# Three row blocks of the gate and up products in one 768-column pass of seven products ahead of the attention, and the down products issued one at a time

## The chip, the cores and the metric

One core of one Trainium2 chip runs the program; the other cores are idle. The metric is the device time of one execution in microseconds (us), and the median of several runs is compared. TensorE (PE) multiplies matrices: it loads a 128x128 stationary tile and streams columns past it (here up to 512 in one matmul) into PSUM, an on-chip accumulator of which the kernel uses eight banks of 512 f32. VectorE (DVE), ScalarE (ACT) and GpSimd (POOL) work on elements; SyncE (SP) issues most of the DMA transfers. Engines run their own instruction lists in order and wait for each other by semaphores.

## The reference, cut to what matters

```python
xn = layernorm(x)                                  # x: 2048 x 512
q  = xn @ wq                                       # 32 heads of 128
o  = softmax(q @ k_cache.T / sqrt(128)) @ v_cache  # per head, 2048 keys
s  = concat(o) @ wo                                # 4096 -> 512
gate, up = xn @ W_gate, xn @ W_up                  # 512 -> 1792 each
h  = relu(gate) * up
g  = silu(h @ W_down)                              # 1792 -> 512
out = x + s * g
```

All inputs are bf16. The two branches (attention s and gated network g) both start from the same normalised rows xn.

## The kernel before, in words

**Row blocks and chunks.** The 2048 rows are four blocks of 512, Q = 0 to 3. The 1792 inner columns of the gated network are FC = 14 chunks of 128. xnT holds xn transposed, with the 512 features as DC = 4 pieces of 128 on the partitions.

**Seven products in place of eight.** Most matrix products are done by Winograd's form of Strassen's method: a 2x2 block product from seven block products (numbered 1 to 7 in the code) instead of eight, with sums of the operands formed beforehand. For the gated network a unit is one chunk k: its gate and up weights are the two rows of the 2x2 scheme (`gu_sums` forms the four weight sums on POOL), two row blocks "lo" and "hi" are its two columns, and the row sums TX (`emit_tx`, on DVE) are shared with the query projection. Each product is two matmuls, one for each half of the feature pieces.

**Order of the work.** Block 0 comes first, plainly (eight matmuls of 512 columns for each chunk): `emit_gate_up(0)`, then `emit_down` with 4 x 14 matmuls, while the layer norm of the other blocks runs in its shadow (`ln_task`, `ln_finish`). Block 2 follows plainly, `emit_gate_up(2)`: 14 chunks x 8 matmuls of 512 columns. Then the attention starts: 32 heads x 4 row blocks make 128 blocks b of eight pairs p. For a pair, PE forms two score tiles (`emit_S_tile`, two matmuls of 512 columns, line 1648), ACT takes the exponential of both (line 1660, 128x1024), and three pairs later PE multiplies with the values (`emit_PV_tile`, eight matmuls of 129 columns, line 1757). Between pairs the list `plan` puts other work of PE: an item takes one of the three two-bank slots of PSUM that the score tiles also use (`emit_M`, `ring_acquire`). Blocks 1 and 3 of the gate and up products are such items: `emit_gu` (line 1199), 14 x 7 products, each 2 matmuls of 512 columns, in attention blocks 2 to 11. Every product is evicted from PSUM by itself: DVE adds it to a running sum (`comb`, line 1205). POOL multiplies gate and up (`gu_h`, lines 1175 and 1177). The weights are loaded a second time, chunk by chunk (`gu_load`), scaled on ACT (`gu_scale`) and summed on POOL.

**Down products.** Blocks 1, 2 and 3 take `emit_d`: seven products, each 14 matmuls of 256 columns (line 1260), in four items of 2, 2, 2 and 1 products. Their places were written by hand in `dplan`: block 2 at attention blocks 0 and 1, block 1 at 12 and 13, block 3 at 14 and 15. `emit_hs` (DVE) forms the sums of h for them, `emit_wd_scale` and `emit_wd_sums` those of W_down.

**Buffers.** Many buffers lie on top of one another in memory and are freed by waits. SP issues DMAs strictly in the order written.

Of the kernel before, what the change touches and what calls it, by code (L numbers as in the profile page):

```python
# [52 lines left out]
def bass_recurrent_scan__mha_block_cached__glu_gated_reglu__prompt_kernel(  # L53
# [63 lines left out]
    with ExitStack() as es:  # L117
# [18 lines left out]
        xnT = S_([128, DC, S], BF16, "xnT")  # L136
# [20 lines left out]
        QT_sb += [at_(xnT_at - base[0] + S + i * 2 * NQ, [128, NQ], BF16, "QT_sb") for i in range(2)]  # L157
# [11 lines left out]
        Wg_sb = at_(67584, [128, DC, F], BF16, "Wg_sb")  # L169
        Wu_sb = at_(81920, [128, DC, F], BF16, "Wu_sb")  # L170
# [4 lines left out]
        def sm_(shape, dt, name):  # L175
# [27 lines left out]
        uB = [at_(61952 + 1024 * i, [128, NQ], BF16, "uB") for i in range(2)]
        gA = [at_(o, [128, NQ], BF16, "gA") for o in (66560, 98304)]
        gB = at_(108544, [128, NQ], BF16, "gB")
        dbuf = {Q: [at_(o, [128, 2, D // 2], F32, "dbuf") for o in os_] for Q, os_ in (
            (2, tuple(range(0, 12288, 2048))), (1, o_w2 + o_sg))}
        dbuf[3] = dbuf[1]
# [20 lines left out]
        hlN = [at_(o, [128, 4, D], BF16, "hlN") for o in (88064, xnT_at - base[0] + 12288)]  # L229
# [18 lines left out]
        sem_gua = newsem()  # L248
        sem_hp = newsem()
# [95 lines left out]

        load_x0(sp, 0)
# [106 lines left out]

        def ln_norm(eng, sem, n, ctok):
            _wait(eng, ctok)
            return sem.sig(
                eng.tensor_scalar(xn_sb[:, n, :], x_sb[:, n, :], rstd[:, n, 0:1], nmr[:, n, 0:1],
                                  op0=ALU.mult, op1=ALU.add))
# [122 lines left out]
        def ln_finish(Q):  # L581
            ns, sqtok = ln_hold.pop("sq")
            ctok = ln_coef(ns, sqtok)
            for n in ns:
                ntok = ln_norm(pool, sem_nm, n, ctok)
                _wait(sp, ntok)
                xt_tok = sem_xq[Q].sig(
                    sp.dma_start_transpose(xnT[:, :, n * 128:(n + 1) * 128], xn_sb[:, n, :]))
# [31 lines left out]
        def emit_tx(k):  # L620
# [3 lines left out]
            b11, b12 = xnT[:, 0:HC, lo], xnT[:, 0:HC, hi]  # L624
            b21, b22 = xnT[:, HC:DC, lo], xnT[:, HC:DC, hi]
# [27 lines left out]
        def gu_scale(k):
            W = W2[k % NW]
            _wait(act, gu_tok[(k, "w")])
            wflat = W[:].rearrange("p c i e -> p (c i e)")
            gu_tok[(k, "s")] = sem_w2s.sig(act.activation(wflat, wflat, ACTF.Copy, scale=GSC))

        def gu_sums(k):
            W, X = W2[k % NW], SG[k % NW]  # L660
            if (k, "s") not in gu_tok:
                gu_scale(k)
            _wait(pool, gu_tok[(k, "s")])
            _wait(pool, gu_tok.get((k - NW, 4)))
            a11, a12 = W[:, 0:HC, 0, :], W[:, HC:DC, 0, :]
            a21, a22 = W[:, 0:HC, 1, :], W[:, HC:DC, 1, :]
# [10 lines left out]
        def emit_sw(pr):  # L677
# [3 lines left out]
            if pr == 0:  # L681
                _wait(pool, tx_tok[(1, 3)])
# [13 lines left out]
            if pr == 1:  # L696
                _wait(pool, glu_done_tok)
# [16 lines left out]
        def finish_gate_up(Q, fc, s, gtok, gu_tok):  # L714
# [4 lines left out]
            rtok = sem_relu.sig(  # L719
                act.activation(gr_sb[gk][:], g_ps, ACTF.Relu, scale=1.0 if Q == 0 else HSC))  # L720
            _wait(dve, gu_tok)
            _wait(dve, rtok)
            h_tok = sem_h.sig(
                dve.tensor_tensor((hT0 if Q == 0 else hT[1])[:, fc, :], gr_sb[gk][:], u_ps, ALU.mult)
            )
            h_done[(Q, fc)] = h_tok
            gr_free[gk] = h_tok
            if s is None:
                (acc_free if Q == 2 else y_bank_free)[:] = [h_tok, h_tok]
            else:  # L730
                ring_tok[s] = [rtok, h_tok]
            if Q == 0:
                ln_task(fc)
            return h_tok

        def emit_gate_up(Q):
            qs = slice(Q * NQ, (Q + 1) * NQ)
            h_tok = None
            for fc in range(FC):
                fs = slice(fc * 128, (fc + 1) * 128)  # L740
                if Q == 0 and fc < HFC:
                    s = half_slots[fc]
                    finish_gate_up(Q, fc, s, half_tok[(fc, 0)], half_tok[(fc, 1)])
                    continue
                if (Q, fc) in ((0, HFC), (2, FC - 2)):
# [4 lines left out]
                g_ps, u_ps = gu_banks(s)  # L750
# [1464 lines left out]
```

## Time and profile before

| what | value |
|---|---|
| median of 3 runs | 1233.03 us (1232.87 to 1233.4) |
| span of the profiled execution, first to last instruction | 1231.4 us |
| own time of the profiled execution | not listed; its span is 1.6 us below the median of the runs |
| PE busy | 1215.4 us (99%) |
| ACT busy | 1043.7 us (85%) |
| DVE busy | 874.6 us (71%) |
| POOL busy | 835.0 us (68%) |
| granted TensorE clock | 1.000 |

Busy time is the time in which an engine executes something. The chain of waits (part 4 of the page) follows the work that ended last back to its start; the view by windows gives busy time of each engine in a stretch; the groups of instructions give the mean duration of one. Mean durations of matmuls are not the pace of a stream: a 512-column matmul is listed with 379 ns, because its end is modelled behind the start of the next. Pace is read from the start times.

### The profile page before, as it was taken

To read this page: it belongs to the slowest core of one execution; us is meant where nothing else is said; L and a number is where in the kernel's file an instruction comes from. 1 tells how busy PE (TensorE), PEld (TensorE's weight loads), DVE (VectorE), ACT (ScalarE), POOL (GpSimd) and SP (SyncE) were. 2 spreads that over 40 slices of the span, in tenths; PEclk is the share of its full clock that TensorE was granted. 3 is DMA by queue.
4 is the path that set the end of the run, shared out by engine and by line. 5 is a ranking of instruction groups with operands and counts; after the bars stand their busy time and mean duration, and the time that the engine had idled before them with its cause. 6 is when DMAs were issued, how large, how long until landed. Compare 5 with 4: busy or idle time off the path is not lost.

```text
span 1231.4 us, 29085 instructions
## 1 busy us (share of the span) xinstructions
PE 1215.4 (99%) x11716; PEld 817.4 (66%) x11926; DVE 874.6 (71%) x1322; ACT 1043.7 (85%) x1114; POOL 835.0 (68%) x945
## 2 busy tenths in 40 slices
PE   9999999999999999999999999999999999999998
PEld 5466666776666666666666666666666666666665
DVE  7668787667676776677666776677676767676587
ACT  4367877668899999999999999999999999999994
POOL 3355876313767867787688776986788767668368
PEclk9999999999999999999999999999999999999999
DMA  9712431323223544246522854265522662248616
GB/s 278 158 31 33 81 80 25 52 48 94 54 52 52 142 125 126 49 94 173 174 38 52 211 155 94 50 154 151 155 52 51 184 191 48 53 104 161 128 35 142
DMA packets 285061, 127.21 MB, mean 103 GB/s; under 512 B 253696, under 2 KB 279552, under 8 KB 280064
## 3 DMA queue, kind: packets, MB, share of 16 engines
q1 hardware_dynamic: 283584, 124.55, 43.2%
q8 instruction: 95, 1.56, 0.6%
q10 hardware_dynamic: 1344, 0.79, 0.2%
q14 instruction: 38, 0.31, 0.1%
HBM read 57.93 MB, written 25.17 MB: 67 GB/s over the span
## 4 chain that ended last, share of the span: by engine, by line
PE 97%; issue 1%; POOL 1%; ACT 0%; DVE 0%; POOLq 0%; DVEq 0%
PE ps_acc L1757 37%; PE ps_r L1648 34%; PE ps_r L1081 5%; PE ps_r L1199 3%; PE ps_r L1545 3%; PE ps_r L1260 3%; PE ps_r L945 2%; PE ps_r L764 2%; PE ps_r L760 2%; PE ps_r L1480 2%; PE ps_acc L863 1%; PE ps_r L1577 1%; PE ps_r L1576 1%; PE ps_r L503 0%; POOL s_acc L1614 0%
## 5 line engine op out<-in xcount | busy, mean ns | idle before, releaser
L1660 ACT ACTIVATE PT<-ps_r 128x1024 bf16<-128x1024 f32 x1024 | 990.5, 1024 | 123.8 <-PE ps_r L1648 109.6
L1757 PEld LDWEIGHTS ps_acc<-V_sb,PT 128*128 128x128 bf16 x8192 | 544.5, 98 | 225.2 <-issue 29.0
L1757 PE MATMUL ps_acc<-V_sb,PT 128*128 128x129 bf16 x8192 | 629.7, 220 | 1.0
L1648 PE MATMUL ps_r<-QT_sb,KT_sb 128*128 128x512 bf16 x1848 | 571.2, 379 | 9.5
L1086 DVE TENSOR_TENSOR UVR<-UVR,ps_r 128x512 f32<-128x512 f32 (+1 forms) x228 | 168.9, 756 | 96.7 <-PE ps_r L1081 91.9
L1648 PEld LDWEIGHTS ps_r<-QT_sb,KT_sb 128*128 128x128 bf16 x2048 | 159.1, 98 | 35.6 <-ACT PT L1660 32.1
L1411 DVE TENSOR_TENSOR s_acc<-s_acc,ps_r 128x1024 f32<-128x1024 f32 x108 | 131.5, 1219 | 27.3 <-PE ps_r L1480 19.3
L1427 DVE TENSOR_TENSOR s_acc<-s_acc,ps_r 128x512 f32<-128x512 f32 x152 | 101.0, 683 | 28.9 <-PE ps_r L1545 23.5
L1680 DVE TENSOR_TENSOR Onorm<-ps_acc,rz_sb 128x512 bf16<-128x512 f32 x127 | 87.8, 691 | 4.4
L1511 POOL TENSOR_TENSOR TI<-OX 128x512 f16<-128x512 f16 x38 | 43.1, 1156 | 69.9 <-issue 68.6
L1046 POOL TENSOR_TENSOR TI<-xn_sb 128x512 f16<-128x512 f16 x48 | 55.9, 1164 | 39.9 <-PE ps_r L1081 39.9
L1086 DVE TENSOR_TENSOR QT_sb<-UVR,ps_r 128x512 bf16<-128x512 f32 x72 | 49.5, 688 | 43.6 <-PE ps_r L1081 41.3
L1677 DVE RECIPROCAL rz_sb<-ps_acc 128x4 f32<-128x4 f32 x127 | 23.2, 183 | 72.4 <-PE ps_acc L1757 70.3
L1511 POOL TENSOR_TENSOR TI<-OT_store 128x512 f16<-128x512 bf16 (+1 forms) x38 | 45.7, 1224 | 32.9 <-PE ps_r L1545 16.1
L1354 POOL TENSOR_TENSOR WX<-Wo_sb 128x512 f16<-128x512 bf16 x7 | 8.1, 1158 | 81.1 <-DVE Wo_sb L1344 42.1
L1046 POOL TENSOR_TENSOR TI<-xn_sb,TI 128x512 f16<-128x512 f16 x48 | 56.0, 1166 | 0.0
L1046 POOL TENSOR_TENSOR TI<-xnT 128x512 f16<-128x512 bf16 x36 | 41.6, 1157 | 13.8 <-PE ps_r L1081 13.8
L1081 PE MATMUL ps_r<-TI,SI 128*128 128x512 f16 x126 | 47.8, 379 | 0.1
L1545 PE MATMUL ps_r<-TI,SI 128*128 128x512 f16 x114 | 43.2, 379 | 0.0
L1046 POOL TENSOR_TENSOR TI<-xnT,TI 128x512 f16<-128x512 bf16 x36 | 41.6, 1156 | 0.0
L1175 POOL TENSOR_SCALAR gB<-gB 128x512 bf16<-128x512 bf16 x14 | 20.8, 1487 | 30.3 <-DVE gB L1205 30.3
L1154 POOL TENSOR_TENSOR UVR<-UVR,UVR 128x512 f32<-128x512 f32 x24 | 29.8, 1274 | 11.7 <-DVE UVR L1086 11.7
(248 smaller groups left out, 1436.8 us busy)
## 6 DMA issues: line engine op xcount, KB each, us to landing
sums<-s_acc SPq DMA_DIRECT2D x20, 1024.0 KB, 4.6
s_acc<-sums SPq DMA_DIRECT2D x18, 1024.0 KB, 5.8
V_sb<-in_A_v_cache_dram SPq DMA_DIRECT2D x32, 512.0 KB, 4.3
Wq_sb<-in_A_wq_dram SPq DMA_DIRECT2D x16, 256.0 KB, 4.4
Wo_sb<-in_A_wo_dram SPq DMA_DIRECT2D x8, 512.0 KB, 3.8
out_dram<-g_sb SPq DMA_DIRECT2D x4, 512.0 KB, 4.7
KR<-sums SPq DMA_DIRECT2D x4, 512.0 KB, 4.5
OT_store<-Onorm SPq DMA_TRANSPOSE x127, 2.7
```

The costliest lines, as they stand in the source:

```text
L1046: return sem_ui.sig(pool.tensor_tensor(dst, x, y, o))
L1081: return sem_up.sig(pe.matmul(dst, lhs, rhs, start=start, stop=stop, skip_group_check=True))
L1086: dve.tensor_tensor(dst, x, ps, ALU.add))
L1199: ins = pe.matmul(ps_r[:, bank, :], L(i), R(i), start=(i == 0), stop=(i == HC - 1))
L1411: t = sem_opa.sig(dve.tensor_copy(dst, sb) if new[0] else dve.tensor_tensor(dst, dst, sb, op))
L1427: t = dve.tensor_tensor(dst, dst, sb, op)
L1511: return sem_oi.sig(pool.tensor_tensor(dst, x, y, o))
L1545: return sem_op.sig(pe.matmul(dst, lhs, rhs, start=start, stop=stop, skip_group_check=True))
L1648: ins = pe.matmul(ps_r[:, 2 * s + tt, :], KT_sb[h % 2][:, t * 128:(t + 1) * 128], QT_sb[qt_slot[(h, Q)]][:], start=True, stop=True)
L1660: act.activation(PT[pb][:], ps_r[:, 2 * s:2 * s + 2, :], ACTF.Exp, scale=scale / WSC)
L1680: dve.tensor_tensor(Onorm[ob][:], o_ap, rz_sb[:].to_broadcast([128, 4, Dh]), ALU.mult))
L1757: ins = pe.matmul(o_ap, PT[pb][:, tt, j * 128:(j + 1) * 128], V_sb[vb][:, t, 0:VW], start=(t == 0 and j % 2 == 0), stop=(t == KT - 1 and j ...
```

## The change

1. **One pass for three row blocks.** Blocks 1, 2 and 3 of the gate and up products are computed together, ahead of the attention. "lo" is block 1 and the first 256 columns of block 2, "hi" is block 3 and the other 256 of block 2, so a product is two matmuls of 512 and two of 256 columns. `emit_tz` forms the row sums TZ for the extra columns. The plain pass `emit_gate_up(2)` and the items of `emit_gu` in the attention are gone.
2. **Sums in PSUM.** Products 1, 6, 5 and 3 accumulate in one PSUM slot "A"; ACT copies the slot out after each (768 columns, f32, the last with relu). Products 7 and 4 share a slot "D", product 2 has a slot "C"; DVE adds the copies to them (`dv`, `gate_low`). DVE also takes the relu of the lower gate and the products gate * up (`gu_h`), which POOL did before. Slots are three of the ring and the two accumulator banks of the values.
3. **A written schedule.** Chunk k issues its product m at step 7k + off[m], so neighbouring chunks interleave; PE waits inside a chunk for ACT's copies and DVE's sums.
4. **Weights stay.** The weights loaded at the start are scaled in place (`gu_scale` during block 0) and used again; the 28 reloads are gone.
5. **Block 2's h goes out.** Its products go through two small buffers to DRAM (14 stores of 128 KB) and come back in one load (`reload_h`) in attention block 6.
6. **Down products** are issued one at a time at 21 places in attention blocks 0 to 15, in the order of blocks 1, 3, 2.
7. **Around it.** The four transposes of a row block become one; the loads of the first heads, of wq and wo are issued elsewhere; W_down is scaled on ACT in seven pieces; the steps of the first query projection are placed anew; the first three score pairs are issued inside the last steps of the pass, and the exponentials of pairs 0, 3 and 4 wait for buffers of the pass.

```diff
-                xt_tok = sem_xq[Q].sig(
-                    sp.dma_start_transpose(xnT[:, :, n * 128:(n + 1) * 128], xn_sb[:, n, :]))
+            xt_ready[Q] = [sem_xq[Q].sig(sp.dma_start_transpose(
+                xnT[:, Q].rearrange("p c (n q) -> p (c n) q", n=4),
+                xn_sb[:, 4 * Q:4 * Q + 4, :].rearrange("p n d -> p (n d)")))]
...
+        def gu_h(k, part, gate, up):
+            t = gu_tok
+            z = slice(part * NX, (part + 1) * NX)
+            _wait_all(dve, [t["g", part, k], t["u", part, k], t.get(("hz", k - 2))])
+            h_done[(3 if part else 1, k)] = sem_hp.sig(
+                dve.tensor_tensor(hT[part][:, k, :], gate[:, 0:NQ], up[:, 0:NQ], ALU.mult))
+            t["f", part, k] = sem_hp.sig(dve.tensor_tensor(hz[k % 2][:, z], gate[:, NQ:], up[:, NQ:], ALU.mult))
+            if part:
+                _wait_all(sp, [t["f", 0, k], t["f", 1, k]])
+                t["hz", k] = sem_hz[k % 2].sig(sp.dma_start(h_keep[k], hz[k % 2]))
+
+        def gate_low(k):
...
+            _wait_all(dve, [gu_tok[(k, 2)], gu_tok["a1", k], gu_tok.get(("f", 0, k - 2))])
+            gu_tok["c11", k] = c = sem_gud.sig(dve.tensor_tensor(
+                g[:], a1b[k % 2][:], gu_ps(s), ALU.add))
...
+            if k > 1:
+                gu_h(k - 2, 1, gB, uB[k % 2])
+            _wait(dve, c)
+            gu_tok["g", 0, k] = sem_gud.sig(dve.tensor_scalar(g[:], g[:], 0.0, None, op0=ALU.max))
...
+                for i in range(HC):
...
+                    for a, r in enumerate(R):
+                        ins = pe.matmul(ps(s)[:, a * NQ:a * NQ + (NX if a else NQ)], L(i), r, start=start and i == 0,
+                                        stop=stop and i == HC - 1, skip_group_check=True)
...
             if m == 1:
+                s = take("A")
...
+                t["a1", k] = cp(a1b[k % 2], s, mm(s, True, False), t.get(("c11", k - 2)))
+            elif m == 6:
...
+                _wait_all(pe, [t[(k, "x")], t["a1", k]])
+                t["a2", k] = cp(a2, s, mm(s, False, False), t.get(("c21", k - 2)))
+            elif m == 5:
...
+                _wait(pe, t["a2", k])
...
+                t["a3"] = cp(a3b, s, mm(s, False, False), t.get("c22"))
+            elif m == 3:
+                s = gu_held["A", k]
+                _wait(pe, t["a3"])
+                t["g", 1, k] = cp(gB, s, mm(s, False, True), t.get(("f", 1, k - 1)), relu=True)
...
             elif m == 7:
+                s = take("D")
+                t["u", 1, k] = t["c22"] = dv(uB[k % 2], a3b, s, mm(s, True, False), t["a3"], t.get(("f", 1, k - 2)))
             else:
+                s = gu_held["D", k]
+                _wait(pe, t["c22"])
+                t["u", 0, k] = t["c21", k] = dv(uA, a2, s, mm(s, False, True), t["a2", k], t.get(("f", 0, k - 1)))
+                give("D", t["c21", k])
+                gu_h(k, 0, gA[k % 2], uA)
...
+            if gp == 0:
+                _wait(act, gu_tok["c11", FC - 1])
+            if gp == NPB - 3:
+                _wait(act, sem_hp.cur())
+            if gp == NPB - 2:
+                _wait_all(act, [s_.cur() for s_ in sem_hz])
...
-        dplan = {2: ((0, 1), (1, 0), (1, 2), (1, 5)),
-                 1: ((12, 3), (13, 0), (13, 3), (13, 6)),
-                 3: ((14, 3), (15, 1), (15, 3), (15, 6))}
+        dpos = [(0, 2), (1, 5), (2, 5), (3, 4), (4, 5), (5, 0), (5, 5), (6, 5), (7, 3), (7, 6), (8, 5), (9, 0), (9, 5),
+                (10, 5), (11, 3), (11, 6), (12, 5), (13, 0), (13, 5), (14, 5), (15, 6)]
...
-        hlast = emit_gate_up(2)
...
+        off = {1: 0, 2: 2, 6: 3, 5: 6, 7: 8, 4: 11, 3: 12}
+        gseq = sorted((7 * k + off[m], k, m) for k in range(FC) for m in off)
...
+        for k in range(2, FC):
+            gside(7 * (k - 1) + 5, gu_sums, k)
...
+            gside(18 + 14 * i, emit_tx, i)
...
+            gside(7 * (2 + i) + 1, emit_wd_scale, i)
+        gside(100, emit_M, [(emit_st, 2, 0, 1, 0)])
+        for gp, t in enumerate((97, 98, 101)):
+            gside(t, emit_S_pair, gp)
...
+        emit_down(h_last, {
+            0: [(gu_scale, FC - 1), (gu_sums, 0), (emit_M, [(emit_st, 2, 0, 0, 0)]), (emit_tx, 4), (emit_tx, 5), (emit_tx, 6), (emit_tx, 7), (emit_tz,)],
+            2: [(gu_begin,), (gu_run, 0, 1)],
+            (3, "mid"): [(gu_sums, 1), (gu_run, 3, 4)]})
+        _wait_all(dve, [y_last["t"], sem_g.cur()])
+        gu_run(1, 3)
+        gu_run(4, 7 * FC - 1)
+        gu_end()
+        gu_run(7 * FC - 1, 7 * FC + 13)
```

More of the change, by code (lines that the diff above doesn't have):

```diff
@@ L155, in at_ @@
             return nc.alloc_sbuf_tensor_at(f"{name}_{_cnt[0]}", shape, dt, offset=base[0] + off)
-        QT_sb += [at_(xnT_at - base[0] + S + i * 2 * NQ, [128, NQ], BF16, "QT_sb") for i in range(2)]
+        QT_sb += [at_(xnT_at - base[0] + 12288 + i * 2 * NQ, [128, NQ], BF16, "QT_sb") for i in range(2)]
         HF = FC // 2
@@ L203, in bass_recurrent_scan__mha_block_cached__glu_gated_reglu__prompt_kernel @@
[L203 to L208, printed above, removed]
+        NX = NQ // 2
+        NP3 = NQ + NX
+        SG = [PT[2][:].rearrange("p a q -> p (a q)").bitcast(F16).rearrange("p (j i e) -> p j i e", j=4, i=DC // 2),
+              at_(99328, [128, 4, DC // 2, 128], F16, "SG")]
@@ L248, in bass_recurrent_scan__mha_block_cached__glu_gated_reglu__prompt_kernel @@
         sem_gua = newsem()
+        sem_tz = newsem()
+        sem_tws = newsem()
+        sem_hz = [newsem(16) for _ in range(2)]
+        sem_h2 = newsem(16)
         sem_hp = newsem()
@@ L456, in ln_norm @@
             return sem.sig(
-                eng.tensor_scalar(xn_sb[:, n, :], x_sb[:, n, :], rstd[:, n, 0:1], nmr[:, n, 0:1],
+                eng.tensor_scalar(xn_view(n), x_sb[:, n, :].rearrange("p (c d) -> p c d", c=DC), rstd[:, n, 0:1], nmr[:, n, 0:1],
                                   op0=ALU.mult, op1=ALU.add))
@@ L659, in gu_sums @@
         def gu_sums(k):
[L660 to L666, printed above, removed]
+            W, X = w_chunk(k), SG[k % 2]
+            _wait_all(pool, [gu_tok[(k, "s")], gu_tok.get((k - 2, 7))])
+            if k == 1:
+                _wait(pool, sem_g.cur())
@@ L857, in emit_down @@
                     pe.wait_ge(sem_wd.h, 16)
-                _wait(pe, y_bank_free[jb])
+                if j < 2:
+                    _wait(pe, y_bank_free[jb])
+                    yps = ps_acc[:, jb, 0:D]
+                else:
+                    if j == 2:
+                        s = ring_acquire()
+                    yps = ps_r[:, 2 * s + jb, 0:D]
                 ins = None
@@ L862, in emit_down @@
                         pe.wait_ge(sem_h.h, h_last_tok[1] - (FC - 1 - fc))
-                    ins = pe.matmul(ps_acc[:, jb, 0:D], hT0[:, fc, j * 128:(j + 1) * 128],
+                    if fc == 10 and (j, "mid") in between:
+                        for fn, *args in between[j, "mid"]:
+                            fn(*args)
+                    ins = pe.matmul(yps, hT0[:, fc, j * 128:(j + 1) * 128],
                                     Wd_sb[:, fc, :], start=(fc == 0), stop=(fc == FC - 1))
@@ L1320, in emit_d @@
-            p4 = prod(4, banks[0])
-            k = comb(y1, c_u, banks[0], ALU.subtract, waits=(p4, d_tok["u"], d_tok["y1"]))
-            d_done[Q] = k
-            out(y1, "y1", 1, 0, 0, k)
+                defer(2, tanh)
+                defer(3, mult)
+            if m == 1:
+                _wait_all(pe, [h_done[(Q, FC - 1)], wd_tok["scale"]])
+            if m == 6:
+                _wait_all(pe, [hs_tok[(Q, 1, 2)], wd_tok["s", 1]])
+            if m == 7:
+                _wait_all(pe, [hs_tok[(Q, 1, 0)], wd_tok["s", 2]])
@@ L1895, in at @@
             plan.setdefault((b, p), []).append(list(items))
-        for step, b, p in ((1, 0, 3), (2, 0, 5)):
-            at(b, p, (emit_st, 2, 0, 1, step))
         GB = G * QB
@@ L2019, in bass_recurrent_scan__mha_block_cached__glu_gated_reglu__prompt_kernel @@
+        side.setdefault((6, 0), []).append((reload_h,))
+        for b in range(2, NBLK):
+            pr, r = (b - 2) // 8 + 1, (b - 2) % 8
             o = osteps.get(b)
```

522 lines of the change are left out of this document (253 added, 269 removed).

## The prediction

> **What bounds the kernel now.** I read the page first: its shares by engine and the chain of work that ended last.
>
> ```profile
> span 1231.4 us, 29085 instructions
> PE 1215.4 (99%) x11716; PEld 817.4 (66%) x11926; DVE 874.6 (71%) x1322; ACT 1043.7 (85%) x1114; POOL 835.0 (68%) x945
> PE 97%; issue 1%; POOL 1%; ACT 0%; DVE 0%; POOLq 0%; DVEq 0%
> ```
>
> The chain is PE for 97% of the span. Then the windows, for the plain pass of block 2, the attention blocks with gate and up items, and the rest (columns: length, busy time of PE, its weight loads, DVE, ACT, POOL):
>
> ```profile
> 43.00:68.00 25.00, 24.89 (x116) 11.36 (x116) 20.79 (x31) 11.28 (x17) 15.24 (x8) 1.00 0.70 151
> 102.00:204.00 102.00, 101.10 (x849) 62.38 (x864) 82.80 (x138) 79.16 (x85) 72.82 (x80) 1.00 0.33 64
> 270.00:1210.00 940.00, 931.10 (x9434) 637.72 (x9602) 660.45 (x953) 859.84 (x892) 682.32 (x786) 1.00 0.45 107
> ```
>
> PE lacks 1% everywhere, at clock 1.00. The chain in order of time says what that is, beside the group of score tiles:
>
> ```profile
> 43.04 0.86 PE ps_r L760 x4
> 43.90 0.86 PE ps_r L764 x4
> ...
> 48.22 0.86 PE ps_r L760 x4
> ...
> 84.69 3.06 PE ps_r L1260 x28
> 87.75 0.45 PE ps_acc L1757 x8
> 88.20 0.05 issue
> ```
> ```profile
> L1648 PE MATMUL ps_r<-QT_sb,KT_sb 128*128 128x512 bf16 x1848 | 571.2, 379 | 9.5
> ```
>
> The gaps are pieces of 0.05 us, and the score tiles number 1848 of the 2048 that 1024 pairs issue: 200 lost records at 0.05 us are the 9.5 us of idle time. They are no stalls. PE is full from the first matmul to the tail, so two things alone move the time: work of PE that goes, and stalls of PE that come. Nothing taken from DVE, ACT, POOL or DMA pays by itself.
>
> **Pace of PE.** Six groups of four take 48.22 - 43.04 = 5.18 us: 0.2158 us for a 512-column matmul. 28 matmuls of 256 columns take 3.06 us: 0.1093 each, with a weight load for each of them.
>
> **Work removed and added on PE.** The plain pass of block 2 goes: 14 x 8 = 112 matmuls of 512, 24.17 us. The 196 matmuls of 512 for blocks 1 and 3 move out of the attention and cost the same. 196 matmuls of 256 columns come: 21.42 us. Down products are 21 x 14 matmuls before and after; query projection and scores don't change. Gain: 24.17 - 21.42 = 2.75 us, if nothing stalls. The pass is then 14 chunks of 14 x (0.2158 + 0.1093) = 4.55 us, 63.7 us in all. The gain cannot be larger: before has no PE idle time to recover.
>
> **The pass in steady state: VectorE.** Its load of one chunk, from these groups, and from starts in order of time:
>
> ```profile
> L1205 DVE TENSOR_TENSOR gA<-gcu,ps_r 128x512 bf16<-128x512 f32 x14 | 9.6, 687 | 5.8 <-PE ps_r L1199 5.1
> L1411 DVE TENSOR_TENSOR s_acc<-s_acc,ps_r 128x1024 f32<-128x1024 f32 x108 | 131.5, 1219 | 27.3 <-PE ps_r L1480 19.3 <-PE ps_r L1545 8.0
> L834 DVE TENSOR_TENSOR HS_sb<-hT 128x1024 f16<-128x1024 f16 x3 | 2.1, 684 | 0.0
> L834 DVE TENSOR_TENSOR HS_sb<-hT 128x768 f16<-128x768 f16 x3 | 1.7, 566 | 0.0
> L1023 DVE TENSOR_SCALAR Wq_sb<-Wq_sb 128x1024 bf16<-128x1024 bf16 x12 | 5.0, 419 | 0.0
> L630 DVE TENSOR_TENSOR xn_sb<-xnT 128x1024 f16<-128x1024 bf16 x2 | 1.4, 684 | 0.0
> ```
> ```profile
> 102.87 0.69 DVE L1205 TENSOR_TENSOR gA<-gcu,ps_r 128x512 bf16<-128x512 f32 x1
> 103.59 0.29 DVE L1218 TENSOR_SCALAR gA<-gA 128x512 bf16<-128x512 bf16 x1
> ...
> 122.05 0.68 DVE L1205 TENSOR_TENSOR uB<-gcv,ps_r 128x512 bf16<-128x512 f32 x1
> 122.65 0.68 DVE L1205 TENSOR_TENSOR gB<-gcv,ps_r 128x512 bf16<-128x512 f32 x1
> ```
>
> In a stream a 512-wide sum out of PSUM takes 0.60 us (122.05 to 122.65), though it lasts 0.68; a dependent successor starts after 0.72. Per column (1219 - 687)/512 = 1.04 ns, so 768 columns take 0.60 + 0.27 = 0.87. Three sums (products 2, 7, 4): 2.6. Gate times up, 16-bit in SBUF: (684 - 566)/256 = 0.46 ns a column, so 512 and 256 columns last 0.45 and 0.33; less 0.08 of overlap each 0.62, for two parts 1.25. The relu over 768: 0.29 + 256 x (419 - 293)/512 = 0.36, less overlap 0.28. One dependent start (sum of product 4, then its multiplication): 0.12. Together 4.25 us of the 4.55: 93%, where before VectorE had 20.79 of 25 and 82.80 of 102. The four row sums placed inside the pass add 4 x 0.65 = 2.6. So 14 x 4.25 + 2.6 = 62.1 against PE's 63.7: slack 1.6 us, 0.11 a chunk.
>
> That takes the SBUF ops at their quiet durations. Beside POOL they are not always quiet:
>
> ```profile
> L1218 DVE TENSOR_SCALAR gA<-gA x14: 293/418/633, 103.6 to 213.1; 128x512 bf16<-128x512 bf16 x14
> ```
> ```profile
> L1218 DVE TENSOR_SCALAR gA<-gA 128x512 bf16<-128x512 bf16 x14 | 6.3, 452 | 0.5
> L670 POOL TENSOR_TENSOR SG<-SG,W 128x256 f16<-128x256 f16 x14 | 9.8, 703 | 0.0
> L1177 POOL TENSOR_TENSOR hT<-gA,uA 128x512 f16<-128x512 bf16 x14 | 16.5, 1179 | 1.2 <-DVE uA L1205 1.1
> ```
>
> The relu of before took 293 to 633 ns, mean 452, where POOL was busy 73 of 102 us. In the pass POOL has only the weight sums, about 4 x 0.70 = 2.8 of 4.55 us, and by the order of waits they start at the end of product 7: while VectorE takes its two PSUM sums (which keep 687 beside POOL). I count one op hit in a chunk, 0.16 us: 14 x 4.41 + 2.6 = 64.3, 0.6 above PE. Bounds: 0 (none hit) and five ops hit, 5 x 0.16 = 0.8: 14 x 5.05 + 2.6 = 73.3, 9.6 above. I take 0.6, nearer to the lower end, because the two engines' bursts fall at different steps.
>
> [...] The spread of the relu agrees with an interference; its mean does not with a block for a whole op, 1.18 us for the multiplications that POOL ran there. [...]
>
> **ScalarE in the pass.**
>
> ```profile
> L1660 ACT ACTIVATE PT<-ps_r 128x1024 bf16<-128x1024 f32 x1024 | 990.5, 1024 | 123.8 <-PE ps_r L1648 109.6 <-remote 0.4
> L720 ACT ACTIVATE gr_sb<-ps_r 128x512 bf16<-128x512 f32 x26 | 15.1, 594 | 18.3 <-PE ps_r L760 17.5 <-PE ps_r L572 0.7
> L657 ACT ACTIVATE W<-W 128x1024 bf16<-128x1024 bf16 x14 | 14.7, 1051 | 0.0
> ```
>
> Between 594 (512) and 1024 (1024) a copy of 768 lasts 0.81: four make 3.2, with a piece of W_down in seven of the chunks 4.3 of 4.55. Product 6 waits for the copy of product 1 with two products (1.3 us) between: 0.81 plus queueing fits by 0.2. No stall, if VectorE keeps up; a late VectorE delays the relu copy and through ACT's order the next copies. In block 0's shadow ACT gets 14 weight scalings: relu and scaling 0.59 + 1.05 = 1.64 a chunk against PE's 8 x 0.2158 = 1.73. The three slots absorb the rest: 0.
>
> **The start of the pass.** Now 43 us is where TX, TZ and the weight sums must be ready, not a chain of its own:
>
> ```profile
> 30.79 12.25 PE L863 MATMUL ps_acc<-Wd_sb,hT 128*128 128x512 bf16 x54
> 31.23 3.03 POOL L457 TENSOR_SCALAR xn_sb<-x_sb,rstd,nmr 128x512 bf16<-128x512 bf16 x4 [2.87 <-DVE nmr L451]
> 34.73 0.49 DVE L875 TENSOR_SCALAR sig_sb<-sig_sb,r 128x512 f32<-128x512 f32 x1 [3.00 <-ACT sig_sb L871]
> ```
> ```profile
> KT_sb<-in_A_k_cache_dram SPq DMA_TRANSPOSE x32, 4.1
> W<-in_B_W_gate_dram SPq DMA_DIRECT2D x14, 128.0 KB, 2.4
> xnT<-xn_sb SPq DMA_TRANSPOSE x16, 2.5
> ```
> ```profile
> 15.15 27.61 SPq L588 DMA_TRANSPOSE xnT<-xn_sb  x16
> ```
>
> The last norm ends at 34.3 us. One transpose of a whole block moves 512 KB as a KT load does, 4.1 us, and queues on SP behind the first KT load: landed at 39. Then VectorE, four row sums x 0.7 and TZ, four half as wide (1.6): 43.4. PE comes to product 6 of chunk 0 at 30.8 + 0.86 (query step) + 52 x 0.2158 (down) + 0.65 = 43.5: level, so I take 0.3 for the hand-overs (0 to 1). The weight sums of chunk 1 wait behind VectorE's last steps for block 0 (buffer under sig_sb): 0.4. Behind VectorE's wait for TX stand its gate products of block 0, and behind them only ScalarE's last tanh. Together 0.7; bounds 0 and 4 (a transpose 4.1 later).
>
> **The change-over to the attention.** The first scores sit in the last steps of the pass. The next query step needs the slot of score pair 0, whose exponential queues on ACT behind the copy of product 5: late by 0.4. Exponential 3 waits for the last gate products, 4 for the last store: 2.4 us for 128 KB, ending some 2.9 us after them, while PE has the last query step, one down product (1.53) and two pairs (0.88 each) to do: late by 0.3. Small ones 0.3. Sum 1.0; bounds 0 and 3.
>
> **Costed at nothing.** POOL's work moved to VectorE (cover: PE's 100% in blocks 2 to 11). Single down products: a pair costs PE 2 x 0.2158 + 0.45 = 0.88, an attention block 7.1 us; ACT 8 x 0.97 (990.5/1024) = 7.7; with a query step of 0.43 to 0.86 and at least one product (1.53) PE has over 9, so ACT stays below it. The reload of h, 1.8 MB, has five blocks of time; the stores wait on SP in front of nothing due. A block left bare would lose 0.6 us.
>
> **Sum.** 1231.4 - 2.75 + 0.6 + 0.7 + 1.0 = 1230.95 span, and 1.6 around it (the median of the runs lies that much above the span): 1232.6 us. That is 0.03% under the median of 1233.03. A measurement here tells about 0.2%, 2.5 us (1230.6 to 1235.5).
>
> **Rivals.** *All waits covered*: 1233.03 - 2.75 = 1230.3. For it: slack exists in each queue on paper, and PE's in-pass waits have 1.3 us of other products in front. Against: two change-overs must both fit exactly. *VectorE becomes the bound*, the case on the other side: place, products 4 and 7, whose PSUM slot waits for VectorE's sum; it decides from 4.36 us of VectorE a chunk on (63.7 - 2.6, over 14). With half the ops hit, 14 x 4.65 + 2.6 = 67.7, 4.0 above PE: 1230.3 + 1.7 + 4.0 = 1236; all five: 1241. [...] For it: slack of 0.11 us a chunk, and the relu's mean. Against: the bursts' order. *The start is late*: block 3's transpose waits behind KT and W_down traffic; 4 us more, 1236. For: before, the transposes of xn kept SP from 15.15 to 42.8 us. Against: they were 16 instructions, and four remain.
>
> **How the numbers follow.** Forecast 0.54 (own range 1230.8 to 1234.5), all covered 0.20, VectorE bound 0.18, late start 0.08. Faster by over 0.2%: all covered and a sliver of the forecast, 0.21. Slower by over 0.2%: three quarters of the VectorE case and half of the late start, 0.18. The range 1230.0 to 1237.0 leaves out 0.05 below and 0.12 above.
>
> **What would show it.** Right: between 45 and 108 us PE shows 512- and 256-column matmuls with under 2 us of waits, a chunk every 4.6 us, and VectorE busy over 90% there; no stalls after the first attention block. Wrong: waits of PE on VectorE in each chunk; pieces of VectorE or ACT in the chain between 45 and 108; PE idle before product 6 of chunk 0; a chain through the store of h before exponential 4; ACT in the chain in blocks 0 to 15; 256-column matmuls away from 0.109 us.

## The result, and the profile after

| kernel | median of the runs | range | ratio to before (95% interval) |
|---|---|---|---|
| before | 1233.08 us | 1232.87 to 1233.4 | |
| changed | 1251.03 us | 1250.61 to 1251.61 | 1.0145 (1.0131 to 1.016) |

The change costs 18 us. The forecast was 1232.6 us in a range of 1230.0 to 1237.0; the result lies 14 us above that range. The profiled execution took 1250.87 us with a span of 1249.6 us.

From the page of the changed kernel: the span, the busy times and the shares of the chain that ended last.

```profile
span 1249.6 us, 29220 instructions
PE 1218.5 (98%) x11798; PEld 825.1 (66%) x12010; DVE 864.1 (69%) x1304; ACT 1075.5 (86%) x1154; POOL 783.4 (63%) x904
PE 94%; issue 2%; DVE 2%; POOL 1%; ACT 1%; DVEq 0%; POOLq 0%; ACTq 0%
```

PE was 97% of the chain and is 94%; DVE and ACT, which stood at 0%, have 2% and 1%. Where that is, the windows tell: ahead of the pass, the pass, its end with the first attention block, and the rest (columns: length, busy time of PE, weight loads, DVE, ACT, POOL; then the granted clock).

```profile
40.00:45.00 5.00, 4.18 (x20) 1.89 (x20) 4.58 (x9) 1.49 (x2) 0.73 (x2) 1.00 1.15 244
45.00:50.00 5.00, 4.39 (x25) 2.16 (x24) 4.48 (x8) 2.60 (x4) 2.79 (x5) 1.00 0.07 12
50.00:104.00 54.00, 53.67 (x322) 30.79 (x329) 51.12 (x97) 41.25 (x54) 31.25 (x48) 1.00 0.08 25
104.00:131.00 27.00, 15.50 (x75) 7.41 (x74) 24.66 (x22) 8.24 (x11) 20.48 (x10) 0.75 0.04 15
204.00:1210.00 1006.00, 996.50 (x10114) 687.61 (x10293) 681.88 (x998) 911.86 (x950) 672.06 (x780) 1.00 0.44 102
```

The same stretch of 27 us in the kernel before:

```profile
104.00:131.00 27.00, 26.73 (x228) 16.64 (x232) 21.83 (x37) 20.00 (x22) 14.99 (x15) 1.00 0.50 89
```

The pass itself, 50 to 104 us, goes as forecast: PE full, DVE at 95%. Ahead of it, from 40 to 50 us, PE lacks 1.4 us. The rest is lost between 104 and 132 us: up to 131 PE is busy 15.50 of 27 us at a mean clock of 0.75, and DVE nearly all the time with only 22 instructions. POOL and DVE there, in order of time (start, duration, engine and line):

```profile
103.72 0.67 POOL L689 TENSOR_TENSOR SG<-WGU,SG 128x256 f16<-128x256 bf16 x1 [0.68 <-PE ps_r L1236]
104.35 3.57 POOL L794 TENSOR_TENSOR WdT<-Wd_sb 128x1792 f16<-128x1792 bf16 x1
108.00 3.62 POOL L796 TENSOR_TENSOR WdT<-Wd_sb,WdT 128x1792 f16<-128x1792 bf16 x1
111.58 3.62 POOL L798 TENSOR_TENSOR Wd<-Wd_sb 128x1792 f16<-128x1792 bf16 x1
115.16 3.74 POOL L800 TENSOR_TENSOR WdT<-WdT,Wd_sb 128x1792 f16<-128x1792 f16 x1
```
```profile
104.69 3.51 DVE L1180 TENSOR_TENSOR hT<-gA,gu 128x512 f16<-128x512 bf16 x1
108.12 3.65 DVE L1181 TENSOR_TENSOR PT<-gA,gu 128x256 f16<-128x256 bf16 x1
111.69 0.94 DVE L1243 TENSOR_TENSOR uB<-ga,ps_r 128x768 bf16<-128x768 f32 x1
113.42 2.06 DVE L1180 TENSOR_TENSOR hT<-gu,uB 128x512 f16<-128x512 bf16 x1
115.41 3.65 DVE L1181 TENSOR_TENSOR PT<-gu,uB 128x256 f16<-128x256 bf16 x1
121.06 0.42 DVE L1180 TENSOR_TENSOR hT<-gA,gu 128x512 f16<-128x512 bf16 x1
121.40 0.28 DVE L1181 TENSOR_TENSOR PT<-gA,gu 128x256 f16<-128x256 bf16 x1
```

The four W_down sums (`emit_wd_sums`) stand in POOL's list right behind the last weight sum of the pass. They are written into the code at attention block 0, but they wait for the scaling of W_down only, so POOL starts them in chunk 11 of the pass. Each takes 3.6 us. A product gate * up of 512 columns on DVE, 0.42 us at 121.06, then takes 3.51; one of 256 columns, 0.28 us at 121.40, takes 3.65. Each ends within 0.3 us of the POOL operation that was running when it started. The sum out of PSUM at 111.69 keeps its 0.94 us. The relu of the lower gate, which has one input, is held as well: 1.18 us at 118.98 beside POOL's line 707, in the pass 0.35. PE waits for DVE's next PSUM sum:

```profile
112.69 0.61 PE L1236 MATMUL ps_r<-xn_sb,WGU 128*128 128x512 f16 x1 [5.85 <-DVE uB L1243]
121.08 1.03 PE L1705 MATMUL ps_r<-QT_sb,KT_sb 128*128 128x512 bf16 x2 [4.37 <-DVE gu L1243]
121.91 0.63 PE L1236 MATMUL ps_r<-xn_sb,SG 128*128 128x512 f16 x1
122.34 0.42 PE L1236 MATMUL ps_r<-TZ,SG 128*128 128x256 f16 x1
131.97 0.38 PE L1705 MATMUL ps_r<-QT_sb,KT_sb 128*128 128x512 bf16 x1 [2.02 <-ACT PT L1723]
```
```profile
119.15 0.81 ACT L1247 ACTIVATE gu<-ps_r 128x768 bf16<-128x768 f32 x1 [11.47 <-DVE PT L1181]
```

The last row is ACT's copy with relu of the other gate, which needs the buffer that the product read and holds up everything behind it on ACT. After each of its two long waits PE runs at half speed: a 512-column matmul takes 122.34 - 121.91 = 0.43 us instead of 0.2158. Windows cut at the waits:

```profile
106.90:112.70 5.80, 0.01 (x1) 0.01 (x1) 5.80 (x4) 0.78 (x1) 5.72 (x3) 0.67 0.00 0
112.70:116.70 4.00, 3.78 (x13) 1.72 (x14) 4.00 (x3) 0.00 (x0) 4.00 (x2) 0.62 0.00 0
121.10:126.00 4.90, 4.90 (x13) 1.88 (x14) 3.37 (x7) 1.51 (x3) 0.59 (x1) 0.51 0.08 27
```

At half clock half of the time is lost: a mean clock of 0.62 over 4.00 us is 1.5 us, 0.51 over 4.90 is 2.4. With the waits, 5.85 + 0.22 + 4.37 + 2.02, the stretch costs 12.5 + 3.9 = 16.4 us.

The kernel before ran the same four sums, 3.57 to 3.60 us each, without loss:

```profile
56.80:71.20 14.40, 14.35 (x68) 6.50 (x67) 9.77 (x16) 6.56 (x10) 14.27 (x5) 1.00 0.13 21
```
```profile
64.01 3.60 POOL L814 TENSOR_TENSOR Wd<-Wd_sb 128x1792 f16<-128x1792 bf16 x1
...
65.52 0.69 DVE L724 TENSOR_TENSOR hT<-gr_sb,ps_r 128x512 f16<-128x512 bf16 x1 [0.51 <-PE ps_r L764]
```

There DVE's operations each took an operand from PSUM (`gr_sb,ps_r`), and PE was busy for 14.35 of 14.40 us. The change put DVE's work with both operands in SBUF, which POOL had done itself, beside POOL's longest operations.

### The profile page after: what moved, and what is told of

Its sections match the earlier page's. It is cut to its first block, busy times and chain, and to the rows that moved or that the text cites. A ratio compares the mean times of both kernels' runs of the same rounds, so it can differ in the third digit from the quotient of the medians.

```text
span 1249.6 us, 29220 instructions
## 1 busy us (share of the span) xinstructions
PE 1218.5 (98%) x11798; PEld 825.1 (66%) x12010; DVE 864.1 (69%) x1304; ACT 1075.5 (86%) x1154; POOL 783.4 (63%) x904
## 4 chain that ended last, share of the span: by engine, by line
PE 94%; issue 2%; DVE 2%; POOL 1%; ACT 1%; DVEq 0%; POOLq 0%; ACTq 0%
PE ps_acc L1820 37%; PE ps_r L1705 34%; PE ps_r L1076 5%; PE ps_r L1602 3%; PE ps_r L1236 3%; PE ps_r L1320 3%; PE ps_r L940 2%; PE ps_r L1537 2%; PE ps_r L773 2%; PE ps_acc L1236 1%; DVE PT L1181 1%; PE ps_r L1634 1%; PE ps_r L1633 1%; PE ps_r L855 0%; PE ps_acc L855 0%
## 5 line engine op out<-in xcount | busy, mean ns | idle before, releaser
L1705 PE MATMUL ps_r<-QT_sb,KT_sb 128*128 128x512 bf16 x1851 | 578.6, 380 | 15.4 <-DVE gu L1243 4.4
L707 POOL TENSOR_SCALAR Wq_sb<-Wq_sb 128x1024 bf16<-128x1024 bf16 x3 | 8.3, 2779 | 120.1 <-DMA Wq_sb<-in_A_wq_dram 120.1
L1329 DVE TENSOR_TENSOR dbuf<-dbuf,ps_r 128x512 f32<-128x512 f32 x21 | 14.2, 687 | 50.0 <-PE ps_r L1320 50.0
```

The source lines that it names most:

```text
L1705: ins = pe.matmul(ps_r[:, 2 * s + tt, :], KT_sb[h % 2][:, t * 128:(t + 1) * 128], QT_sb[qt_slot[(h, Q)]][:], start=True, stop=True)
```

## Experiments

Theory A: a POOL operation holds off, until it ends, a DVE operation with both operands in SBUF. Its rivals: B, the two share a path by halves, so that only the amount of POOL's work counts; C, POOL is not the cause, the last chunks lose their time to PSUM slots and to the scores and query steps woven into them. The kernel before measured 1232.8 to 1232.9 us beside each of these runs.

### The sums behind the pass: e1_sums_late

```diff
-                _wait_all(pool, [wd_tok["scale"], sem_nm.cur()])
+                _wait_all(pool, [wd_tok["scale"], sem_nm.cur(), sem_hp.cur()])
```

> The four W_down sums stay on POOL, but wait for VectorE's last gate product of the pass. Theory A (a POOL operation of 3.6 us holds off, for all of its length, a VectorE operation with both operands in SBUF): VectorE's gate products of the last chunks are back at 0.42 and 0.28 us, PE's waits of 5.85 and 4.37 us and the stretches at half clock go, worth 12.2 us idle and some 4 at half clock; against that POOL is now late, 110 + 14.4 + 2.8 + 2.9 = 130, and the half sums of h fall beside its sums in block 1, which may cost 0 to 5: 1235 to 1240. Theory C (POOL is not the cause, the last chunks lose their time to PSUM slots and to the scores and query steps woven into them): about 1250, with the same two waits.

Measured: 1237.86 us (1236.62 to 1240.13), 13.2 under the changed kernel; C falls. PE's two long waits and the half clock are gone. The products of a group, in the view of the groups of instructions, have a mean of 431 ns (the changed kernel: 673):

```profile
L1180 DVE TENSOR_TENSOR hT<-gA,gu 128x512 f16<-128x512 bf16 x14 | 6.0, 431 | 0.5
```

The new collision came where it was expected, in attention block 1, with the half sums of h (`emit_hs`, 0.69 us in the quiet):

```profile
126.04 3.69 DVE L818 TENSOR_TENSOR HS_sb<-hT 128x1024 f16<-128x1024 f16 x1
```
```profile
125.60 3.59 POOL L800 TENSOR_TENSOR WdT<-WdT,Wd_sb 128x1792 f16<-128x1792 f16 x1
```
```profile
135.62 0.61 PE L1705 MATMUL ps_r<-QT_sb,KT_sb 128*128 128x512 bf16 x2 [2.41 <-DVE dbuf L1329]
```

### The sums in pieces: e2_sums_split

```diff
-                t = pool.tensor_tensor(WdT[:, 0], b12, b11, ALU.subtract)
+                for i in range(HF):
+                    t = sem_wdt.sig(pool.tensor_tensor(WdT[:, 0][:, i], b12[:, i], b11[:, i], ALU.subtract))
```

and the same for the other three sums.

> The four W_down sums stay where they are on POOL, each in seven pieces of 256 columns, 28 x 0.62 = 17.4 us instead of 14.5. Theory A: a VectorE operation now waits for one piece at most, 0.3 to 0.62 on each of five in a chunk, 1.5 to 3.1 a chunk for the last three or four chunks, of which VectorE's slack takes 0.3: 4 to 9 us instead of 16 and hardly a stretch at half clock: 1238 to 1244. Theory B (POOL and VectorE share a path by halves, so that only the amount of POOL's work counts): as slow as with whole sums, 1251 to 1254. Theory C: 1250.

Measured: 1239.66 us (1238.29 to 1240.19), inside the bounds of A; B, with 1251 to 1254, falls, although POOL's work in this place grew from 14.6 to 19.1 us. One sum in its seven pieces, and two products beside it:

```profile
104.08 4.91 POOL L795 TENSOR_TENSOR WdT<-Wd_sb 128x256 f16<-128x256 bf16 x7
```
```profile
104.96 0.75 DVE L1184 TENSOR_TENSOR PT<-gA,gu 128x256 f16<-128x256 bf16 x1
...
111.24 0.89 DVE L1183 TENSOR_TENSOR hT<-gu,uB 128x512 f16<-128x512 bf16 x1
```

A product now waits for one piece: 0.75 instead of 3.65 us. And the pieces beside products take 0.70 us each, against 0.62 in the stream of the weight sums. In both runs the price of a meeting for DVE goes with the length of the POOL operation that is running (3.65 us beside a sum of 3.62, 0.75 beside a piece of 0.70), not with the amount of POOL's work, which grew. It is not nothing: PE still waits 0.93, 1.05 and 2.38 us, and behind the last of these its granted clock is 0.50 from 120.54 to 123.95 us.

### The sums on DVE: e3_sums_vector, e4_sums_scale_vector

```diff
-                t = pool.tensor_tensor(WdT[:, 0], b12, b11, ALU.subtract)
+                t = dve.tensor_tensor(WdT[:, 0], b12, b11, ALU.subtract)
...
-            side.setdefault((0, i), []).append((emit_wd_sums, i))
+            side.setdefault((0, 4 + i), []).append((emit_wd_sums, i))
```

In e4_sums_scale_vector DVE also scales the second query weights (line 707, on POOL until then).

> The four W_down sums move to VectorE, in the second half of the first attention block: four of about 1.0 us by the half sums of h (0.684 for 1024 columns, 0.46 ns for each further one), where VectorE had 4.4 us idle between 130 and 137. POOL's scaling of the second query weights, 2.80 us, comes up to 104.35. Theory A: one gate product waits behind that one operation, about 2.4 us, PE loses about 2: 1251 - 16.4 - 1.0 + 2 = 1235 to 1236. Theory C: 1250.

> As e3_sums_vector, and the scaling of the second query weights on VectorE as well (0.42 us), so that POOL has no long operation beside the gate products. Theory A: 2 us under e3_sums_vector, 1233 to 1234, with no wait of PE over 1 us between 50 and 125 and the clock at 1.00. Theory C: 1250.

Measured: 1240.44 us (1240.03 to 1242.23) and 1238.66 us (1238.49 to 1240.37). The order of the two and C's fall are as expected, the sizes are not: 5 us more each. Three things show in e3_sums_vector. Its POOL operation of 2.78 us holds DVE for 1.3 us at most:

```profile
104.27 2.78 POOL L707 TENSOR_SCALAR Wq_sb<-Wq_sb 128x1024 bf16<-128x1024 bf16 x1
...
114.30 0.85 POOL L716 TENSOR_TENSOR SW<-Wq_sb 128x256 f16<-128x256 bf16 x1
```
```profile
104.60 0.98 DVE L1180 TENSOR_TENSOR hT<-gA,gu 128x512 f16<-128x512 bf16 x1
105.51 0.28 DVE L1181 TENSOR_TENSOR PT<-gA,gu 128x256 f16<-128x256 bf16 x1
...
114.55 0.75 DVE L1181 TENSOR_TENSOR PT<-gA,gu 128x256 f16<-128x256 bf16 x1
```

The product at 105.51 runs at full speed while line 707 is still listed as running: for this operation with one input the listed span is longer than its hold. Second, the sums of the query weights (lines 715 to 720, from 113.67 on) meet the last products of the pass, 0.73, 0.75, 0.88 and 0.75 us instead of 0.42 and 0.28. Exponential 3 waits for these, and PE 2.02 us for it. The changed kernel's wait of 2.02 us at 131.97 is the same meeting. Third, three W_down sums of 1.08 us on DVE in a row delay the normalisation of the first heads' values (Onorm), on which PE waited 1.94 us here and 2.28 in e4_sums_scale_vector:

```profile
127.54 1.02 PE L1824 MATMUL ps_acc<-V_sb,PT 128*128 128x129 bf16 x8 [2.28 <-DVE Onorm L1747]
```

Both waits were followed by a stretch at half clock (in e3_sums_vector the clock is 0.50 from 130.17 to 133.58 us), which costs 1.7 us each; the wait of 2.41 us in e1_sums_late was not (windows of e4_sums_scale_vector and of e1_sums_late; the clock is the number behind POOL's):

```profile
122.00:131.00 9.00, 6.67 (x53) 4.47 (x52) 8.79 (x14) 4.11 (x5) 3.31 (x4) 0.81 0.08 15
```
```profile
131.00:140.00 9.00, 6.54 (x64) 4.15 (x63) 8.21 (x14) 5.17 (x6) 5.40 (x5) 1.00 0.08 15
```

### No collision left: e5_spread, and three edits to what remains

```diff
-            side.setdefault((0, i), []).append((emit_wd_sums, i))
+            side.setdefault(((0, 4), (1, 7), (2, 7), (3, 6))[i], []).append((emit_wd_sums, i))
...
             else:
+                if pr == 1:
+                    _wait(pool, sem_hp.cur())
                 k = sem_sw.sig(pool.tensor_scalar(wflat, wflat, WSC, None, op0=ALU.mult))
```

with the sums on DVE as in e3_sums_vector.

> No long POOL operation and no burst on VectorE: the four W_down sums on VectorE, one each in attention blocks 0, 1, 2 and 3, and POOL's scaling of the second query weights waits for VectorE's last gate product. Against e1_sums_late the half sum of h in block 1 that waited 3.69 us behind POOL, and PE's wait of 2.41 us behind it, go, and against e4_sums_scale_vector the wait of 2.28 us and the stretch at half clock. Theory A (what is left above the forecast in those two runs is these collisions, and the small waits at the start): 1237.9 - 2.4 = 1235.5, or 1234 by the profiled run of e1_sums_late (its block 16 starts 3.5 us later than in the kernel before). If something else in blocks 0 to 3 holds PE (the rival), the time stays at 1237 to 1239.

Measured: 1236.35 us (1234.97 to 1237.22), 14.7 under the changed kernel, but 0.9 above the 1235.5 of Theory A and 0.7 below the rival's 1237, so the median alone does not decide. To see how much of the collision is gone, the profiles are compared where the work ahead is the same: the second exponential of these groups of two is the first of attention block 16 (the kernel before, the changed one, e5_spread):

```profile
268.81 1.92 ACT L1660 ACTIVATE PT<-ps_r 128x1024 bf16<-128x1024 f32 x2
```
```profile
285.47 1.96 ACT L1723 ACTIVATE PT<-ps_r 128x1024 bf16<-128x1024 f32 x2
```
```profile
269.81 1.96 ACT L1725 ACTIVATE PT<-ps_r 128x1024 bf16<-128x1024 f32 x2
```

The changed kernel is 16.66 us behind there, e5_spread 1.00. The 15.66 us between them are the 16.4 of waits and half clock counted above, less the 0.28 and 0.30 us that PE still waits for exponentials at the change-over, to within 0.2 us. The other versions add up to within 0.2 us as well: by the same exponential e1_sums_late is 2.4 us behind e5_spread (its wait of 2.41), e3_sums_vector 5.6 (2.02 + 1.94 and 1.7 at half clock) and e4_sums_scale_vector 4.1 (2.28 and 1.7). That closes the account of the loss up to block 16.

The next three edits each took one of the small waits left, one on top of the other: e6_start_sums puts the row sums at the start in the order in which PE needs them, e7_start_order moves product 6 of chunk 0 behind the down products of block 0, e8_scale_split has W_down scaled in 14 pieces. The lines of the three edits that matter:

```diff
-            0: [..., (emit_tx, 4), (emit_tx, 5), (emit_tx, 6), (emit_tx, 7), (emit_tz,)],
+            0: [..., (emit_tx, 4), (emit_tz, 0), (emit_tx, 6), (emit_tz, 1), (emit_tx, 5), (emit_tz, 2), (emit_tx, 7), (emit_tz, 3)],
...
-            (3, "mid"): [(gu_sums, 1), (gu_run, 3, 4)]})
+            (3, "mid"): [(gu_sums, 1)]})
...
-        gu_run(1, 3)
+        gu_run(3, 4)
+        gu_run(1, 3)
...
-            w = Wd_sb[:, 2 * k:2 * k + 2, :].rearrange("p c d -> p (c d)")
+            w = Wd_sb[:, k:k + 1, :].rearrange("p c d -> p (c d)")
```

> As e5_spread, with VectorE's row sums at the start of the pass in the order in which PE's products need them, and PE waiting for those of product 6 alone at product 6. The wait of 0.77 us ahead of product 6 of chunk 0 goes: 0.8 us under e5_spread. If that wait is set by the transposes and not by the order of the sums, no difference.

> As e6_start_sums, with product 6 of chunk 0 behind the last down product of block 0 instead of inside it, so that tanh and the gate of that row block, which free the PSUM slot of product 7, come 0.65 us earlier. The waits of 0.39 and 0.22 us at 48.9 and 49.9 go, and product 5 may wait 0.2 for the copy of product 6: 0.2 to 0.6 us under e6_start_sums.

> As e7_start_order, with ScalarE's scaling of W_down in 14 pieces of 512 columns, one a chunk, instead of 7 of 1024. In the kernel after, chunks with such a piece took 4.67 and 4.63 us and the ones without 4.57; the piece of 1.08 us delays the next copy, one of about 0.6 fits into the 1.03 us that ScalarE has free there: 0.6 to 0.8 us under e7_start_order. If VectorE's four row sums for the queries make these chunks longer, and not ScalarE, no difference.

Measured: 1236.38, 1236.34 and 1235.67 us. By the first exponential of block 16 they gained 0.36, 0.07 and 0.29 us, less than expected. With 0.77 us gone, 0.37 and 0.22 stayed; with those gone, PE waited 0.75 us for ScalarE's copy of product 6. The 0.29 us of e8_scale_split were there before its edit acts: product 1 of chunk 0 starts at 40.75 instead of 41.21 us. Its chunks kept their 4.67 and 4.63 us from one relu to the next, and the ones from chunk 9 on their 4.57, though all of them now carry a piece of the scaling: what makes chunks 1 to 8 longer is not ScalarE. It fits the four row sums on DVE, placed in chunks 2, 4, 6 and 8: by PE's own starts every second chunk there takes 4.73 us and the others 4.57. No run moves these sums.

### Behind block 16: e9_sp_pad, e10_after_sp_pad, e12_first_chunks

e8_scale_split is level with the kernel before at block 16 (0.29 us behind) and yet ends 2.8 us later by the medians.

```diff
+            if (bq, pq) == (40, 5):
+                for j in range(48):
+                    _wait(sp, (sem_nm, sem_g)[j % 2].cur())
```

e10_after_sp_pad is the changed kernel with these lines; e12_first_chunks is e9_sp_pad with `gu_run(7, 8)` ahead of `gu_run(4, 7)`.

> As e8_scale_split, with 24 instructions more on SP that wait for what has long been reached, in attention block 40. Open is why e8_scale_split, whose block 127 starts 0.8 us later than in the kernel before, ends 2.8 us later. Theory P: between SP's 335th and 336th instruction stands a stop of up to 2 us, in which its next code is loaded (1.3 us from one transpose of the tail to the next became 3.2 in e5_spread); the changed kernel has 24 SP instructions fewer than the kernel before, and so this stop has moved into the tail. With 24 more it is back ahead of the tail: 1235.7 - 1.5 to 2 = 1233.7 to 1234.2, and the transposes of the tail follow each other by 1.3 us. Theory Q (the tail is longer by chance, or by other places in SBUF or DRAM): 1235.7, and the stop stays.

> The changed kernel as it is, with the same 24 SP instructions in block 40 and nothing else. Theory P: its stop in the tail was shorter, 2.1 us between two transposes instead of 1.3, so 0.8 to 1.5 us under its 1251.0: 1249.5 to 1250.2. Theory Q: 1251.0.

> As e9_sp_pad, with product 1 of chunk 1 ahead of product 5 of chunk 0, so that PE has 0.65 us of work while ScalarE copies product 6 of chunk 0. PE's wait of 0.91 us there shrinks to 0.2 to 0.3: 0.6 us under e9_sp_pad, and with Theory P 1233.1 to 1233.6, level with the kernel before. If the copies on ScalarE only move their delay to product 7, no difference to e9_sp_pad.

Measured: 1235.31 us (1234.77 to 1237.67), 1250.50 us (1249.6 to 1250.94) and 1235.60 us (1234.31 to 1236.41). The four transposes on SP at the start of the tail, in the kernel before, e8_scale_split and e9_sp_pad:

```profile
1207.74 5.21 SPq L1800 DMA_TRANSPOSE FO<-gT  x4
```
```profile
1208.53 5.77 SPq L1874 DMA_TRANSPOSE FO<-gT  x4
```
```profile
1208.69 5.62 SPq L1874 DMA_TRANSPOSE FO<-gT  x4
```

The 24 instructions more did not move the stop: 5.62 us for four transposes stand against 5.77 without them, and 5.89 in e10_after_sp_pad against 6.02 in the changed kernel. The 7.05 us of e5_spread had become 5.77 in e8_scale_split with no SP instruction added. The medians moved by 0.36 and 0.53 us, which runs that scatter over 1.3 us and more don't tell from nothing. Theory P falls: the stop is still in the tail, and the gain is not there. In the traces of the kernel before and the changed one a packet of the instruction queue q8 falls between two transposes of the tail that start 2.21 and 2.08 us apart (at 1218.0 and 1224.9 us); that it causes the stop is not shown. e12_first_chunks, too, made no difference; PE's wait for the copy of product 6 went from 0.64 us in e9_sp_pad to 0.39, and one of 0.22 came further down. No version beats the kernel before; the best lie 0.2% above it (e12_first_chunks: 1.002, interval 1.0011 to 1.0028).

From block 16 to the end the profiled executions lose 0.3 us (e2_sums_split) to 3.2 us (e7_start_order) against the kernel before, the changed kernel 1.5. What costs this stays open. The profiles of e5_spread and the versions built on it lose 0.35 us at block 21, 0.3 to 0.8 in block 127 and up to 1.9 us behind its last exponential (e7_start_order; nothing there in e12_first_chunks), and the repaired versions' runs scatter over 2 to 5.6 us where those of the kernel before lie within 1.6. No run separates the new DRAM buffer, the moved buffers in SBUF and the shifted positions in the engines' code.

## Why the prediction was wrong, by its own steps

**What bounds the kernel, the pace, the gain.** Right. Chunks 9 to 11 took 4.57 us against 4.55 worked out, and the 2.75 us fit the repaired versions, though no run measures them alone: e8_scale_split reaches block 16 0.3 us behind the kernel before, so some 3.0 us must have been lost there. Of these 1.5 us are seen as waits of PE (0.91, 0.28 and 0.31) and 0.9 as longer chunks; 0.6 are not located.

**The pass in steady state.** Right in size: 0.6 us above PE was forecast; chunks 1 to 9 took 4.65 on average, about 0.9 us over the pass. The hit of 0.16 us that it counts in each chunk is seen in seven of them: a product of 512 columns took 0.58 us beside a weight sum instead of 0.42. The excess is not even: it sits in every second chunk, as the row sums do.

**The step that failed** is the sentence "In the pass POOL has only the weight sums, about 4 x 0.70 = 2.8 of 4.55 us". It took the place in which `emit_wd_sums` is written, attention block 0, for the time at which it runs. POOL's list was not followed past the last weight sum: four operations of 3.6 us come next, what they wait for was met in the pass, and DVE's last three chunks still had to go through. They cost 14.3 of the 16.4 us: the waits of 5.85, 0.22 and 4.37 us and 3.9 at half clock (of the 4.37, about 0.8 are the relu held beside line 707). The other 2.02 are the meeting with the query weight sums. The same step stands once more under "Costed at nothing": "POOL's work moved to VectorE" was priced by PE's cover where it came from, blocks 2 to 11, and not by what runs beside it where it goes; it is these products that were held. The list of where the changed work stands on every queue must include the operations whose code stays and whose calls the diff moves.

**The block that was weighed and set aside.** The products stopped for whole POOL operations: 3.51 and 3.65 us for 0.42 and 0.28. With the W_down sums in pieces of 0.70 us (e2_sums_split) the wait is a piece, 0.75 us for 0.28; line 707 held a product for at most 1.3 of its 2.78 us (e3_sums_vector). The prediction had set aside a block for a whole operation because the relu of the kernel before had a mean of 452 ns beside operations of 1.18 us. Read one by one, these relus, which have one input, show the hold. Five of the 14 met no operation of POOL and took 0.29 us. Nine met one, and each of the nine ended 0.13 to 0.15 us behind it, as here in the kernel before:

```profile
109.78 0.63 DVE L1218 TENSOR_SCALAR gA<-gA 128x512 bf16<-128x512 bf16 x1
```
```profile
109.11 1.15 POOL L1177 TENSOR_TENSOR hT<-gB,uB 128x512 f16<-128x512 bf16 x1
```

They began late in POOL's operation and waited for its rest, which a mean cannot show. The bounds of the forecast counted hits of 0.16 us, at most five in a chunk, where the meeting was with operations of 3.6 us.

**The clock.** No step had it. A wait of PE was priced at its length; two of them (5.85 and 4.37 us) cost 3.9 us more, since PE came back at half speed.

**ScalarE.** "A late VectorE delays the relu copy and through ACT's order the next copies": so it went; the relu copy waited 11.47 us for DVE's product, and behind it on ACT stood the next copy and the first exponential.

**The start.** Forecast 0.7, measured 0.77 + 0.39 + 0.22 = 1.4 us, within its bounds of 0 and 4. The 0.77 is at product 6 of chunk 0, as named, the 0.39 at the slot that the last gate of block 0 frees.

**The change-over.** Forecast 1.0, bounds 0 and 3; 0.28 and 0.30 us of waits in e5_spread, 2.02 in the changed kernel, which are POOL's query weight sums and not the store of h.

**Costed at nothing.** The POOL work moved to DVE is the loss itself, as said above. Single down products and the reload of h can have cost at most the 0.6 us not located up to block 16. Behind it the forecast had no term, and the 0.3 to 3.2 us lost there stay open.

**Rivals.** All waits covered: no. A late start by the transposes: no; the 0.77 us went when the row sums were put in another order. VectorE as the bound: in part. The first long wait is at a product 4, as named, the second at a score pair whose slot the sum of a product 4 frees; but DVE was held off from outside, not full.

## What to carry to other kernels

Before work moves from one engine to another, follow the list of every engine past the edited place and ask what runs earlier than it is written, because its waits are met. Two-operand SBUF work on DVE and long POOL operations on SBUF did not go side by side here (3.65 us for 0.28): cut the POOL operation short, give it a wait, or let DVE do it (1.08 us for 3.6). A wait of PE can cost more than its length, as the clock can fall with it: 1.7 us more for one of 1.94 us in e3_sums_vector. And a mean over operations that meet a neighbour now and then says nothing of one meeting: set the end of each beside the end of what it met.

## What the runs showed of the hardware that was not expected

- Beside the W_down sums of the changed kernel DVE's products waited for the rest of POOL's operation: up to 3.65 us for 0.28 us of work, while sums with one operand in PSUM kept 0.94 us. The in-place relu, with one input, waited too: 0.63 us for 0.29 in the kernel before.
- POOL's scaling of 128x1024 (one input, in place) is listed with 2.78 us in e3_sums_vector but let DVE go after 1.3 at most.
- PE's granted clock went to 0.50 with waits of 5.85 and 4.37 us, and after those of 2.38 us in e2_sums_split, 1.94 in e3_sums_vector and 2.28 in e4_sums_scale_vector; it stayed at 1.00 after 2.41 us in e1_sums_late and after 2.02 in the changed kernel. In e4_sums_scale_vector it is 0.81 over nine us, 0.5 for 3.4 of them (127.58 to 130.99 us). So the length of a wait alone did not decide whether the clock fell; what did is not shown.
